# Attention, MoE and a second MoE on one core: w_in with one scale per column half, q and k of the first units as rows of two tokens, two 256-token tiles in a PSUM bank

## The chip, the cores and the metric

The kernel runs on one core of a Trainium2 chip. The metric is the device time of one execution in microseconds; smaller is better. Of several executions the median counts.

## The reference

`reference()` chains three blocks over 3072 tokens. B, H, S, D are 4, 8, 768, 64.

```
for each chunk of 32 queries:                # per batch and head
    k_full = [8 memory keys, k of 16 tokens left, the chunk, 8 tokens right]
    a = softmax(q_c @ k_full.T / sqrt(D));   out_c = a @ v_full
x = out as 3072 x 512
h = x @ w_in                                 # 512 x 2048
g = max(h, 0) + alpha * min(h, 0)
x = g @ w_out                                # 2048 x 512
out = ((x @ w_a) * (x @ w_b)) @ w_out2       # 512 x 1536 twice, 1536 x 512
```

All weights come as 64-bit floating-point numbers in device memory.

## The kernel before, in words

**Weights.** Each weight is loaded as pairs of 32-bit words and rebuilt in f32 on the chip (`chunk`): rebase (L557, L559), shift (L568, L573), magnitude (L579), sign (L587), sizes (L595, L598). Then it is split into a high f16 part (`split_hi`, L370 on POOL or L372 on ACT) and a low f16 part (`split_lo`, L376, always on DVE), both after multiplying by a power of two, the scale. A product of two such pairs takes three f16 matmuls (`gemm3`, L1004 to L1006). w_in comes in 8 chunks of 256 columns, w_out in 8 chunks of 64. All of w_in has one scale, taken from the largest of the 8 chunks' sizes (`scale_w1`, L517); so no chunk of w_in can be split before the last one has its sizes. Each w_out chunk has its own scale. `scale` (L328) turns the sizes with one TensorE transpose (L334) and has four small DVE rows (L339, L343, L347, L350).

**Attention.** 24 units of 128 tokens. For each, SP loads k (L729), q (L777) and v (L791); a row of q or k is one token of one head, 256 bytes. TensorE turns k (L733) and q (L805), four f32 transposes of 128x128 each; ACT and DVE copy the keys to `kT` (L668, L670); the scores are L829, their row maximum on DVE L845 (or L835 and L845), the exponentials on ACT L855, the norm L871, the turn of the probabilities L888, their product with the values L902. In the first 8 units the mask is added by TensorE (L820).

**First MoE.** Tokens go in blocks: two of 256 (two units each), then five of 512. `x_block` (L957) scales x and splits it (`xhl`). `gemm1` (L1008) makes, for each of the 16 row tiles m of h, 12 matmuls into one of four PSUM banks `mm`, then g: `below` on ACT (L1028), `both` on DVE (L1031), the high part on ACT (L1037), the low part on DVE (L1040). `gemm2` (L1057) makes the four column tiles of the output, each in four groups of 12 matmuls, one group per quarter of w_out's rows. The columns of tile 3 are w_out chunks 6 and 7.

**The order.** Nothing runs as written: the class `Schedule` collects every operation with an engine, a cost, a rank and the buffers it reads, writes and holds, and `emit` then writes the program by list scheduling on those costs. Each engine executes its instructions in the order in which they were written. Where `emit` foresees TensorE idle for more than 1.5 us it puts dummy matmuls there (`warm`: L354, L881, L1021). Slots limit how far work runs ahead: 4 banks for `mm`, 2 for `pair` (the turns of k, the scores), 3 `raw` and 2 `w32` slots for weights in preparation, 2 each for q, k and v. Chunks 1 to 3 of w_in wait for their scale in the buffer of g (`ghl`), chunks 4 to 7 in that of w_out (`w_96` in the rows of the order).

**After phase 1** the second MoE follows with a scheme of seven products per 2x2 block of matrices; the change does not touch it.

Of the kernel before, what the change touches and what calls it, by code (L numbers as in the profile page):

```python
# [8 lines left out]
F32 = mybir.dt.float32  # L9
# [10 lines left out]
P = 128  # L20
# [192 lines left out]
def tile_attention_moe_moe2(  # L213
# [81 lines left out]
    s_w1, inv_w1 = col(), col()  # L295
# [204 lines left out]
    in_x, in_g = Buf(raw_slots), Buf(ghl_slots)  # L500

# [13 lines left out]
    am_w1, am1_w1 = col(NC1), col()  # L515

    def scale_w1(rank):  # L517


        def largest():  # L520
            nc.vector.tensor_reduce(out=am1_w1, in_=am_w1, axis=AX.X, op=ALU.max)

        sd.op("DVE", took["largest"], rank, largest, [("amw1", c) for c in range(NC1)], [("amw1", -1)])
        after = [
            lambda: nc.vector.tensor_tensor(out=iy0, in0=als, in1=inv_w1, op=ALU.mult),
            lambda: nc.vector.tensor_scalar(iy0, iy0, 1.0 / E1, None, op0=ALU.mult),
        ]
        scale(lambda: am1_w1, s_w1, inv_w1, [("amw1", -1), ("alpha", 0)], [("s_w1", 0)], after=after)

    def chunk(nm, c, w, kt, cw, rank, load_rank):  # L530
# [32 lines left out]
        def shifted(e):  # L563
# [8 lines left out]
            b = b.rearrange("p (g f) -> p g f", g=2 * kt) if nm == "w1" else b  # L572
# [46 lines left out]
        def scaled():  # L619
            src = [rk, ("s_w1", 0)] if nm == "w1" else [(w32, 0), (key + "s", 0)]  # L620
            if nm in ("w1", "w2"):
                wh, wl = (w1h, w1l) if nm == "w1" else (w2h, w2l)
# [4 lines left out]

                def hi_(e):
                    split_hi(f(), wh[:, :, cols], s, e)

                def lo_():
                    split_lo(f(), wh[:, :, cols], wl[:, :, cols], s)
# [76 lines left out]

    def keys(iu, rank):  # L710
# [3 lines left out]
        kw, pk = Buf(kw_slots), Buf(pair_slots)  # L714
# [31 lines left out]
        sd.op("SP", 1.5, max(iu - 1, 0) * 2.0 + (0.05 if iu else 0.0), load, (), [(kw, 0)])  # L746
        sd.op("PE", 4 * pe(P, 2), rank - 5000, turn, [(kw, 0)], [(pk, 0)])
# [10 lines left out]
    def attention(iu, b, u, x32, part, am, rank):  # L758
# [6 lines left out]
        qt, vw = Buf(qt_slots), Buf(vw_slots)  # L765
# [9 lines left out]
        def load_q():  # L775
            t0 = 2 * u * QB
            nc.sync.dma_start(out=qt.tile, in_=q[b, :, t0 : t0 + P, :].rearrange("h p d -> p h d"))  # L777
# [19 lines left out]
        sd.op("SP", 1.5, lr, load_q, (), [(qt, 0)])  # L797
# [5 lines left out]
        def q_turn():  # L803
            for g in range(HP):
# [113 lines left out]
        sd.op("PE", 4 * pe(P, 2), prank, q_turn, [(qt, 0)], [(pq, 0)], holds=[qT])  # L918
# [38 lines left out]
    def x_block(jb, x32, xhl, c0, rank):  # L957
# [9 lines left out]
        def largest():  # L967
# [15 lines left out]
            [(f"sx{jb}", 0), ("s_w1", 0)], [(f"iy{jb}", 0)],  # L983
# [15 lines left out]
    def gemm3(ps, ops, first=True, last=True):  # L999
# [3 lines left out]
        for i, (lh, ll, rh, rl) in enumerate(ops):  # L1003
            nc.tensor.matmul(out=ps, lhsT=lh, rhs=rh, start=first and i == 0, stop=False)  # L1004
# [139 lines left out]
    for jb, (x32, xhl, ghl, c0, ar, r1, r2) in enumerate(place):  # L1144
# [3 lines left out]
        for m in range(KF1):  # L1148
            gemm1(jb, m, xhl, ghl, c0, n, r1)
# [337 lines left out]
```

## Time and profile before

| | |
|---|---|
| median of 3 runs | 1159.72 us (1158.94 to 1162.37) |
| profiled execution | 1160.92 us, span 1159.1 us, mean granted clock 0.989 |
| TensorE busy | 1124.0 us, 97% of the span, 9253 matmuls |
| DVE busy | 846.7 us, 73% |
| ACT busy | 569.6 us, 49% |
| POOL busy | 279.8 us, 24% |
| DMA | 147.83 MB, 128 GB/s over the span |

The profile is one execution, so its own time is the one to which sums of its rows belong; the span is the part of it that the trace covers. An engine's share of the span is a mean over stages which differ: attention and weight preparation in the first 180 us, matmuls alone later.

### The profile page before, as it was taken

How to read it: one execution, taken by the hardware profiler on the slowest of the kernel's cores; microseconds unless marked ns; L12 is line 12 of the kernel's file. 1: busy time of each engine (PE TensorE's matmuls, PEld its weight loads, DVE VectorE, ACT ScalarE, POOL GpSimd, SP SyncE). 2: the span in 40 equal slices, each digit the busy share in tenths (PEclk: the TensorE clock that was granted, in tenths of full speed). 3: DMA queues.
4: the chain of work that ended last, by engine and by line, in shares of the span. 5: the costliest groups of instructions: out<-in, count | busy, mean ns of one | idle time of the engine just before them, and what ended most of it. 6: DMA issues, size and time to landing. Idle time of an engine off the chain costs nothing.

```text
span 1159.1 us, 22903 instructions
## 1 busy us (share of the span) xinstructions
PE 1124.0 (97%) x9253; PEld 807.8 (70%) x9253; DVE 846.7 (73%) x1472; ACT 569.6 (49%) x1263; POOL 279.8 (24%) x339
## 2 busy tenths in 40 slices
PE   5688999999999999999999999999999999999998
PEld 3477886555555545444444588888888888888887
DVE  5899898877787789654352287976976967958982
ACT  4878767866686676444141122533433433424340
POOL 3432632112112202301200010323332342332610
PEclk9789999999999999999999999999999999999999
DMA  9847655536636543461103162612613504505301
GB/s 269 239 96 172 159 138 151 164 90 184 196 96 170 171 138 99 157 250 46 46 1 136 49 202 68 203 54 101 207 41 115 189 26 146 165 19 177 97 36 38
DMA packets 149874, 147.83 MB, mean 128 GB/s; under 512 B 91385, under 2 KB 127241, under 8 KB 149769
## 3 DMA queue, kind: packets, MB, share of 16 engines
q1 hardware_dynamic: 149768, 146.37, 41.5%
q8 instruction: 73, 1.20, 0.4%
q14 instruction: 33, 0.26, 0.1%
HBM read 117.25 MB, written 29.10 MB: 126 GB/s over the span
## 4 chain that ended last, share of the span: by engine, by line
PE 86%; DVE 9%; ACT 2%; POOL 1%; issue 1%; SPq 1%; DMA 0%; ACTq 0%; DVEq 0%; POOLq 0%
PE mm L1004 27%; PE mm L1006 27%; PE mm L1005 27%; PE mm L902 2%; PE pair L888 2%; DVE w L376 1%; PE pair L829 1%; DVE w L579 1%; DVE w L587 1%; POOL w L370 1%; DVE g L1031 1%; PE mm L805 1%; DVE ghl L1040 1%; PE pair L733 1%; ACT sm L855 1%
## 5 line engine op out<-in xcount | busy, mean ns | idle before, releaser
L1004 PE MATMUL mm<-xhl,w 128*128 128x512 f16 (+1 forms) x448 | 157.6, 352 | 4.3 <-DVE g L1031 3.7
L1005 PE MATMUL mm<-xhl,w 128*128 128x512 f16 (+1 forms) x448 | 157.5, 352 | 1.9 <-DVE xhl L376 1.9
L1006 PE MATMUL mm<-xhl,w 128*128 128x512 f16 (+1 forms) x448 | 157.6, 352 | 0.0
L1004 PE MATMUL mm<-ghl,w 128*128 128x512 f16 (+1 forms) x448 | 156.3, 349 | 0.0
L1006 PE MATMUL mm<-ghl,w 128*128 128x512 f16 (+1 forms) x448 | 156.2, 349 | 0.0
L1005 PE MATMUL mm<-ghl,w 128*128 128x512 f16 (+1 forms) x448 | 156.2, 349 | 0.0
L1004 PE MATMUL mm<-units,w1b 128*128 128x256 f16 x560 | 152.6, 273 | 0.0
L1006 PE MATMUL mm<-units,w1b 128*128 128x256 f16 x560 | 152.6, 273 | 0.0
L1005 PE MATMUL mm<-units,w1b 128*128 128x256 f16 x560 | 152.6, 273 | 0.0
L1006 PEld LDWEIGHTS <-w 128*128 128x128 f16 x896 | 88.1, 98 | 81.1 <-issue 2.1
L1005 PEld LDWEIGHTS <-w 128*128 128x128 f16 x896 | 88.2, 98 | 78.1 <-issue 5.0
L1004 PEld LDWEIGHTS <-w 128*128 128x128 f16 x896 | 88.4, 99 | 75.2
L1005 PE MATMUL mm<-w2b,w1b 128*128 128x256 f16 x504 | 137.4, 273 | 0.0
L1004 PE MATMUL mm<-w2b,w1b 128*128 128x256 f16 x504 | 137.4, 273 | 0.0
L1006 PE MATMUL mm<-w2b,w1b 128*128 128x256 f16 x504 | 137.4, 273 | 0.0
L1004 PEld LDWEIGHTS <-w1b 128*128 128x128 f16 x1064 | 104.1, 98 | 12.1
L1006 PEld LDWEIGHTS <-w1b 128*128 128x128 f16 x1064 | 104.1, 98 | 12.1
L1005 PEld LDWEIGHTS <-w1b 128*128 128x128 f16 x1064 | 104.1, 98 | 12.1
L1031 DVE SCALAR_TENSOR_TENSOR g<-g,columns,mm 128x512 f32<-128x512 f32 (+1 forms) x112 | 73.7, 666 | 26.0 <-ACT g L1028 25.9
L1028 ACT ACTIVATE g<-mm 128x512 f32<-128x512 f32 (+1 forms) x112 | 59.4, 536 | 63.1 <-PE mm L1006 61.7
L1040 DVE SCALAR_TENSOR_TENSOR ghl<-g,ghl 128x512 f16<-128x512 f32 (+1 forms) x112 | 70.2, 637 | 25.3 <-ACT ghl L1037 24.8
L1037 ACT ACTIVATE ghl<-g 128x512 f16<-128x512 f32 (+1 forms) x112 | 62.5, 569 | 30.9 <-DVE g L1031 30.6
(306 smaller groups left out, 2339.0 us busy)
## 6 DMA issues: line engine op xcount, KB each, us to landing
w1b<-wa_d SPq DMA_DIRECT2D x26, 896.0 KB
w1b<-wb_d SPq DMA_DIRECT2D x26, 896.0 KB
raw<-in_moe_w_out_dram SPq DMA_DIRECT2D x8, 1024.0 KB
vw<-in_v_dram SPq DMA_DIRECT2D x40, 176.0 KB
kw<-in_k_dram SPq DMA_DIRECT2D x24, 256.0 KB
qt<-in_q_dram SPq DMA_DIRECT2D x24, 256.0 KB
raw<-in_moe_w_a_dram SPq DMA_DIRECT2D x12, 512.0 KB
raw<-in_moe_w_b_dram SPq DMA_DIRECT2D x12, 512.0 KB
```

Of the source, the lines that this page charges most:

```text
L370: nc.gpsimd.tensor_scalar(hi, src, s, None, op0=ALU.mult)
L376: nc.vector.scalar_tensor_tensor(out=lo, in0=src, scalar=s, in1=hi, op0=ALU.mult, op1=ALU.subtract)
L579: nc.vector.scalar_tensor_tensor(out=f, in0=a, scalar=3 if by["e"] == "ACT" else 29, in1=b, op0=ALU.logical_shift_left if by["e"] == "ACT" ...
L888: nc.tensor.transpose(out=heads(pp, P)[:KW, o, g], in_=sm.tile[:, o, g], identity=ident)
L902: nc.tensor.matmul(out=out[64 * o : 64 * o + 64, g, c], lhsT=vw.tile[:, j, 2 * g + o], rhs=pT.tile[:, o, g, c], start=True, stop=True,)
L1004: nc.tensor.matmul(out=ps, lhsT=lh, rhs=rh, start=first and i == 0, stop=False)
L1005: nc.tensor.matmul(out=ps, lhsT=lh, rhs=rl, start=False, stop=False)
L1006: nc.tensor.matmul(out=ps, lhsT=ll, rhs=rh, start=False, stop=last and i == n - 1)
L1028: nc.scalar.activation(out=g.tile[:, :n], in_=ps.tile[:, :n], func=ACTF.Relu, scale=-1.0)
L1031: nc.vector.scalar_tensor_tensor(out=g.tile[:, :n], in0=g.tile[:, :n], scalar=fal[:, m : m + 1], in1=ps.tile[:, :n], op0=ALU.mult, op1=ALU ...
L1037: nc.scalar.activation(out=ghl.tile[:, 0, m, d], in_=g.tile[:, :n], func=ACTF.Copy, scale=E1)
L1040: nc.vector.scalar_tensor_tensor(out=ghl.tile[:, 1, m, d], in0=g.tile[:, :n], scalar=E1, in1=ghl.tile[:, 0, m, d], op0=ALU.mult, op1=ALU.s ...
```

## The change

Four things, all in the first phase.

(a) w_in gets two scales, one for each half of its columns (4 chunks each). `scale_w1` makes both; four small DVE rows (`ratios`) form r_w1, what each half's scale lacks to the common one. Each w_out chunk multiplies its own scale by r_w1 (one small DVE row, L656 of the new kernel), and its rows are split in two halves, each with its own factor: two high parts and two low parts of 512 per chunk for one each of 1024.

(b) The f16 parts of w_in are stored chunk by chunk (`w1c`) and those of w_out by column tile (`w2m`), so that one chunk's write is contiguous where it was 8 pieces of 128.

(c) q and k of units 0 to 3 are loaded as rows of two tokens, 512 bytes, into 64 partitions of two `raw` slots (`load_wide`), one slot for two units. `turn_wide` turns them with 16 ordinary f32 matmuls with an identity of 64x64 each, where there were four transposes of 128x128; the output goes to every second column of PSUM, even and odd tokens apart.

(d) In the two blocks of 256 tokens two row tiles m share a PSUM bank (`gemm1_pair`): one `below`, one high part on ACT and one low part on DVE for each pair, 512 wide; `both` stays at 256 because its factor differs by m.

The core of the diff:

```diff
-    s_w1, inv_w1 = col(), col()
+    s_w1, inv_w1, r_w1 = col(2), col(2), col(2)
-    w1h, w1l = w1.rearrange("p (x k f) -> x p k f", x=2, k=KD)
+    w1c = w1.rearrange("p (c x k f) -> c x p k f", c=NC1, x=2, k=KD)
-    w2h, w2l = w2.rearrange("p (x k f) -> x p k f", x=2, k=KF1)
+    w2m = w2.rearrange("p (m x k f) -> m x p k f", m=KD, x=2, k=KF1)
...
+        for h in range(2):
+            def largest(h=h):
+                nc.vector.tensor_reduce(
+                    out=am1_w1[:, h : h + 1], in_=am_w1[:, h * NH : (h + 1) * NH], axis=AX.X, op=ALU.max
+                )
...
+            scale(
+                lambda h=h: am1_w1[:, h : h + 1], s_w1[:, h : h + 1], inv_w1[:, h : h + 1],
+                [("amw1", -1 - h)], [("s_w1", h)],
+            )
+        def ratios():
+            nc.vector.tensor_reduce(out=imax, in_=inv_w1, axis=AX.X, op=ALU.max)
+            nc.vector.reciprocal(out=smin, in_=imax)
+            nc.vector.tensor_scalar(r_w1, inv_w1, smin, None, op0=ALU.mult)
+            nc.vector.tensor_scalar(iy0, imax, als, 1.0 / E1, op0=ALU.mult, op1=ALU.mult)
...
+                halves = [(slice(0, kt), s)] if nm == "w1" else [(slice(0, kt // 2), sr[:, :1]), (slice(kt // 2, kt), sr[:, 1:])]
                 def lo_():
-                    split_lo(f(), wh[:, :, cols], wl[:, :, cols], s)
+                    for ks, x in halves:
+                        split_lo(f()[:, ks], wh[:, ks], wl[:, ks], x)
+                        lambda: nc.vector.tensor_scalar(sr, r_w1, s, None, op0=ALU.mult),
...
+    def load_wide(i, src, iu):
+        (t, r), (b, u) = wide(iu, i), units[iu]
+        nc.sync.dma_start(
+            out=t[r].rearrange("p h e d -> p h (e d)"),
+            in_=src[b, :, u * P : (u + 1) * P, :].rearrange("h (p e) d -> p h (e d)", e=2),
+        )
+    def turn_wide(i, out, iu):
+        t, r = wide(iu, i)
+        out = out.rearrange("p (g t e) -> p g t e", g=HP, e=2)
+        for g in range(HP):
+            for e in range(2):
+                for o in range(2):
+                    nc.tensor.matmul(
+                        out=out[64 * o : 64 * o + 64, g, :, e], lhsT=t[r, 2 * g + o, e], rhs=ident[r, r],
+                        start=True, stop=True,
+                    )
...
-        sd.op("SP", 1.5, lr, load_q, (), [(qt, 0)])
+        sd.op("SP", 0.8 if iu < 4 else 1.5, lr, load_q, (), [qkey])
...
+    def gemm1_pair(jb, m, xhl, ghl, c0, rank):
+        for x in range(2):
+            def product(x=x, c=c, wh=wh, wl=wl):
+                xh, xl = xhl.tile[:, 0, :, d], xhl.tile[:, 1, :, d]
+                gemm3(
+                    halves(ps.tile)[:, x], [(wh[:, i, c], wl[:, i, c], xh[:, i, :], xl[:, i, :]) for i in range(KD)],
+                    first=x == 0, more=True,
+                )
+        sd.op("ACT", act(TB), er, below, [(ps, 0)], [(g, 0), (g, 1)])
+        for x in range(2):
+            sd.op("DVE", dve(HT, pointers=1), er, lambda x=x: both(x), [(ps, 0), ("alpha", 0)], [(g, x)])
+        sd.op("ACT", act(TB), er, hi_, [(g, 0), (g, 1)], [(ghl, ("h", m, c0))])
+        sd.op("DVE", dve(TB), er, lo_, [(g, 0), (g, 1), (ghl, ("h", m, c0))], [(ghl, (m + x, c0)) for x in range(2)], port=True)
```

Since `emit` sets the order from costs and slots, the whole order of the first phase shifts. Three places of it follow; the rows are instructions of one engine in program order, with the line, the operation, the tiles and the shape, and x16 for sixteen of them in a row.

TensorE, from the turn of unit 0's probabilities (L888, now L947) to unit 1's scores (L829, now L888); before:

```order
L888 MATMUL pair<-ident,sm 96x128 x8
L902 MATMUL mm<-pT,vw 64x64 x16
L805 MATMUL mm<-ident,qt 128x128 x4
L733 MATMUL pair<-ident,kw 128x128 x4
L820 LDWEIGHTS ident_92
L820 MATMUL pair<-mask_90,ident_92 128x384
L820 LDWEIGHTS ident_92
L820 MATMUL pair<-mask_90,ident_92 128x384
L829 MATMUL pair<-kT,qT 64x96 x16
```

and in the changed kernel:

```order
L947 MATMUL pair<-ident,sm 96x128 x8
L754 MATMUL mm<-ident,raw 64x64 x16
L961 MATMUL mm<-pT,vw 64x64 x16
L754 MATMUL pair<-ident,raw 64x64 x16
L879 LDWEIGHTS ident_92
L879 MATMUL pair<-mask_90,ident_92 128x384
L879 LDWEIGHTS ident_92
L879 MATMUL pair<-mask_90,ident_92 128x384
L888 MATMUL pair<-kT,qT 64x96 x16
```

The turn of q for unit 1 stood behind the product with the values and stands ahead of it now; the turn of k for unit 2 stays ahead of unit 1's scores. Four transposes have become sixteen matmuls in both.

DVE, around the row maximum of unit 1 (`nm`); before:

```order
L911 TENSOR_REDUCE columns<-x_302 128x1
L587 SCALAR_TENSOR_TENSOR ghl<-ghl,w_95 128x1024
L668 COPY kT<-pair 128x4x80
L587 SCALAR_TENSOR_TENSOR ghl<-ghl,w_95 128x1024
L845 TENSOR_REDUCE nm<-pair 128x8
L568 TENSOR_SCALAR w_95<-w_95 128x8x128
L579 SCALAR_TENSOR_TENSOR w_95<-w_96,w_95 128x8x128
```

and in the changed kernel, up to the first rows of the next chunk:

```order
L970 TENSOR_REDUCE columns<-x_353 128x1
L695 COPY kT<-pair 128x4x16
L695 COPY kT<-pair 128x4x8
L602 SCALAR_TENSOR_TENSOR ghl<-ghl,w_95 128x1024 x2
L904 TENSOR_REDUCE nm<-pair 128x8
L526 TENSOR_REDUCE columns<-columns 128x1
L340 TENSOR_REDUCE m<-mm 128x1
L344 TENSOR_SCALAR m<-m 128x1
L348 TENSOR_SCALAR columns<-m 128x1
L351 RECIPROCAL columns<-columns 128x1
L584 TENSOR_SCALAR w_95<-w_95 128x1024
L594 SCALAR_TENSOR_TENSOR w_95<-w_96,w_95 128x1024
```

The two signs of w_in chunks (L587, now L602) stand next to each other ahead of the maximum, behind the copies of the keys. Behind the maximum come the largest size of w_in's first half (L526) and the rows of its scale (L340 to L351); before, the one scale of w_in stands behind the first xhl.

DVE, the end of w_out: the last chunks' low parts (`w_96` is the buffer of w_out, with numbered tiles as sources); before:

```order
L350 RECIPROCAL columns<-columns 128x1
L668 COPY kT<-pair 128x4x72
L602 COPY columns<-columns 64x1
L668 COPY kT<-pair 128x4x8
L1076 TENSOR_TENSOR columns<-columns 128x1 x2
L376 SCALAR_TENSOR_TENSOR w_96<-w_1801,columns,w_96 128x16x64
L376 SCALAR_TENSOR_TENSOR w_96<-w_1854,columns,w_96 128x16x64
```

and in the changed kernel:

```order
L351 RECIPROCAL columns<-columns 128x1
L617 COPY columns<-columns 64x1
L1192 TENSOR_TENSOR columns<-columns 128x1 x2
L656 TENSOR_SCALAR columns<-columns 128x2
L584 TENSOR_SCALAR w_2092<-w_2092 128x1024
L594 SCALAR_TENSOR_TENSOR w_2092<-raw,w_2092 128x1024
L970 TENSOR_REDUCE columns<-x_1365 128x1
L377 SCALAR_TENSOR_TENSOR w_96<-w_1938,columns,w_96 128x8x64 x2
```

The low parts of the last two chunks stood next to each other, 1024 each (16x64). Now the last chunk stands alone, in two halves of 512 (8x64), with a shift and a magnitude (L584, L594) of the next weight and a row of sizes (L970) between its factor (L656) and its low part. On POOL the order has 14 of the long operations on weights (L370, L557) up to there where it had 18.

## Rows read from the trace of the kernel before

**Rows 1.** Page, busy tenths in 40 slices; then windows: busy us and instructions per engine.

```profile
PE   5688999999999999999999999999999999999998
...
59.00:180.00 121.00, 112.00 (x1263) 94.83 (x1263) 112.04 (x236) 93.36 (x268) 49.70 (x28) 0.97 0.56 137
180.00:240.00 60.00, 60.00 (x520) 35.36 (x517) 49.12 (x86) 45.35 (x120) 6.95 (x11) 1.00 0.56 156
```

**Rows 2.** Waits, TensorE 59 to 180 us, DVE 33 to 160 us: total, times, longest.

```profile
PE mm L1004 <- DVE g L1031: 3.7, 2, 2.8
PE mm L1005 <- DVE xhl L376: 1.9, 1, 1.9
...
DVE w L376 <- POOL w L370: 2.2, 3, 1.0
...
DVE w L376 <- ACT w L372: 0.8, 1, 0.8
```

**Rows 3.** Chain that ended last, pieces in order: start us, us, what.

```profile
8.80 3.98 DMA kw<-in_k_dram
...
154.21 2.85 POOL w L370
157.09 2.48 DVE w L376 x2
```

**Rows 4.** Timeline of TensorE at 160.7 us: start us, us, instruction.

```profile
160.72 0.27 PE L1004 MATMUL mm<-ghl,w 128*128 128x256 f16 x1
```

**Rows 5.** DMA traffic from 0 to 20 us in slices of half a microsecond.

```profile
GB/s 0 0 0 14 88 156 217 340 397 381 375 299 276 267 209 184 184 190 115 75 203 264 195 186 271 336 397 373 389 385 397 401 401 393 385 389 393 389 385 382
```

**Rows 6.** Timeline of TensorE, 12 to 45 us; in brackets the idle time before.

```profile
12.83 1.12 PE L733 MATMUL pair<-ident,kw 128*128 128x128 f32 x4 [2.10 <-DMA kw<-in_k_dram]
...
15.43 1.54 PE L829 MATMUL pair<-kT,qT 64*64 64x96 f32 x28 [0.33 <-DVE kT L668]
...
25.80 2.57 PE L902 MATMUL mm<-pT,vw 96*64 96x64 f32 x32 [0.78 <-DVE pT L668]
...
43.11 1.98 PE L902 MATMUL mm<-pT,vw 96*64 96x64 f32 x32 [1.39 <-ACT pT L670]
```

**Rows 7.** Timeline of DVE, row maxima of units 0 and 1, one scale.

```profile
17.03 0.96 DVE L845 TENSOR_REDUCE nm<-pair 128x8 f32<-128x768 f32 x1 [1.65 <-PE pair L829]
...
33.05 0.96 DVE L845 TENSOR_REDUCE nm<-pair 128x8 f32<-128x768 f32 x1 [0.23 <-PE pair L829]
...
53.87 0.29 DVE L339 TENSOR_REDUCE m<-mm 128x1 f32<-128x128 f32 x1 [0.42 <-PE mm L334]
```

**Rows 8.** DVE timeline; then groups by form, busy us, mean ns; DVE, then ACT.

```profile
10.97 1.21 DVE L587 SCALAR_TENSOR_TENSOR raw<-raw,w 128x1024 int32<-128x1024 int32 x1
...
19.88 2.01 DVE L587 SCALAR_TENSOR_TENSOR ghl<-ghl,w 128x1024 int32<-128x1024 int32 x1
...
82.24 0.75 DVE L1040 SCALAR_TENSOR_TENSOR ghl<-g,ghl 128x256 f16<-128x256 f32 x2
...
L1040 DVE SCALAR_TENSOR_TENSOR ghl<-g,ghl 128x512 f16<-128x512 f32 x80 | 56.3, 711 | 24.9 <-ACT ghl L1037 24.4
...
L376 DVE SCALAR_TENSOR_TENSOR xhl<-x,columns,xhl 128x512 f16<-128x512 f32 x24 | 17.4, 766 | 0.0
...
L376 DVE SCALAR_TENSOR_TENSOR w<-w,columns,w 128x1024 f16<-128x1024 f32 x12 | 16.3, 1376 | 2.2 <-POOL w L370 1.5 <-ACT w L372 0.8
...
L1040 DVE SCALAR_TENSOR_TENSOR ghl<-g,ghl 128x256 f16<-128x256 f32 x32 | 13.9, 451 | 0.4 <-ACT ghl L1037 0.4
...
L568 DVE TENSOR_SCALAR w<-w 128x1024 int32<-128x1024 int32 x14 | 10.0, 714 | 1.1 <-ACT w L559 1.1
...
L343 DVE TENSOR_SCALAR m<-m 128x1 int32<-128x1 int32 x47 | 7.1, 151 | 1.1
...
L372 ACT ACTIVATE w<-w,columns 128x1024 f16<-128x1024 f32 x5 | 6.0, 1217 | 0.7 <-DVE columns L350 0.7
```

**Rows 9.** Group of TensorE by form: busy us, mean ns of one.

```profile
L829 PE MATMUL pair<-kT,qT 64*64 64x96 f32 x768 | 24.5, 260 | 1.4 <-ACT kT L670 0.9 <-DVE kT L668 0.3
```

More of the change, by code (lines that the diff above doesn't have):

```diff
@@ L500, in tile_attention_moe_moe2 @@
     in_x, in_g = Buf(raw_slots), Buf(ghl_slots)
+    wide_qk = [Buf(raw_slots) for _ in range(2)]
     def raw_key(c):
@@ L513, in raw_tile @@
         return t[:, c * n : (c + 1) * n].bitcast(I32).rearrange("p (f t) -> p f t", t=2)
-    am_w1, am1_w1 = col(NC1), col()
+    am_w1, am1_w1 = col(NC1), col(2)
+    NH = NC1 // 2
     def scale_w1(rank):
[L520 to L528, printed above, removed]
+        for h in range(2):
[3 more added lines that the diff above has]
+                )
+            sd.op(
+                "DVE", took["largest"], rank, largest, [("amw1", c) for c in range(h * NH, (h + 1) * NH)],
+                [("amw1", -1 - h)],
+            )
[8 more added lines that the diff above has]
+            nc.vector.tensor_scalar(iy0, imax, als, 1.0 / E1, op0=ALU.mult, op1=ALU.mult)
+        sd.op("DVE", 4 * took["tiny"], rank, ratios, [("s_w1", 0), ("s_w1", 1), ("alpha", 0)], [("r_w1", 0)])
     def chunk(nm, c, w, kt, cw, rank, load_rank):
@@ L997, in x_block, with gemm3 @@
         return iy
[L999 removed]
+    def gemm3(ps, ops, first=True, last=True, more=False):
         n = len(ops)
         for i, (lh, ll, rh, rl) in enumerate(ops):
[L1004 to L1006 removed]
+            nc.tensor.matmul(out=ps, lhsT=lh, rhs=rh, start=first and i == 0, stop=False, skip_group_check=more)
+            nc.tensor.matmul(out=ps, lhsT=lh, rhs=rl, start=False, stop=False, skip_group_check=more)
+            nc.tensor.matmul(out=ps, lhsT=ll, rhs=rh, start=False, stop=last and i == n - 1, skip_group_check=more)
     def gemm1(jb, m, xhl, ghl, c0, n, rank):
         ps, g = Buf(mm_slots), Buf(g_slots)
[L1010 removed]
+        c = slice(m % GR * P, (m % GR + 1) * P)
+        wh, wl = w1c[m // GR, 0], w1c[m // GR, 1]
         d = slice(c0, c0 + n)
@@ L1016, in product @@
                 ps.tile[:, :n],
-                [(w1h[:, i, c], w1l[:, i, c], xh[:, i, :], xl[:, i, :]) for i in range(KD)],
+                [(wh[:, i, c], wl[:, i, c], xh[:, i, :], xl[:, i, :]) for i in range(KD)],
             )
@@ L1147, in tile_attention_moe_moe2 @@
         iy = x_block(jb, x32, xhl, c0, ar)
-        for m in range(KF1):
-            gemm1(jb, m, xhl, ghl, c0, n, r1)
+        for m in range(0, KF1, 2 if n == HT else 1):
+            if n == HT:
+                gemm1_pair(jb, m, xhl, ghl, c0, r1)
+            else:
+                gemm1(jb, m, xhl, ghl, c0, n, r1)
         for m in range(KD):
```

86 lines of the change are left out of this document (68 added, 18 removed).

## The prediction

> **What bounds the kernel now.** I read the stretches of the span first, since the share of busy time hides the stages [rows 1]. From 180 us on TensorE hardly pauses: 60.00 us busy of 60, and nine tenths or more in every later slice of the span but the last. So whatever the change does, it must do by bringing TensorE's work before 180 us to an earlier or later end. Between 59 and 180 us TensorE is busy 112.00 of 121 us, so 9.0 us of idle time is all that can be won there; DVE is busy 112.04 us in the same stretch, so it is as full as TensorE.
>
> The waits and the chain name the links. From 59 to 180 us the products of the first GEMM wait 3.7 us for g and 1.9 us for xhl, both written by DVE. DVE in turn waits, from 33 to 160 us, 2.2 us for POOL's and 0.8 us for ACT's rounding of weights [rows 2]. The chain that ended last runs at its front through the load of k (8.80 to 12.83 us), and before GEMM2's last column block through POOL's rounding of a w_out chunk (2.85 us) and DVE's two low parts behind it, which end at 157.09 + 2.48 = 159.57 us [rows 3]. The first product that needs them, by the order the 577th of the two GEMMs, starts at 160.72 us [rows 4]. So only 1.1 us lies between the end of the weights' preparation and their use: TensorE's stream and DVE's w_out chain are both critical, and a gain on one is worth little more than 1 us without the other. That decides the forecast.
>
> I split the change at two marks: N, the row maximum of unit 1 on DVE (33.05 us in the rows), and M, the first product with the last two w_out chunks (160.72 us).
>
> **Part 1: loads and turns of q and k, up to N.** The wide loads move the same 256 KB each. While the narrow ones run, the DMA moves 184 to 209 GB/s, and with w_in alone 373 to 401 [rows 5]: 256 KB are 1.40 us at 187 and 0.68 us at 385, so each gains 0.7 us. By the order three of them (k0, q0, k1) lie ahead of unit 0's scores, 2.1 us together. The turns for k1 started 2.10 us late for that load, but the maximum of unit 0 had DVE idle only 1.65 us [rows 6, 7], and DVE had other work for the rest: I take 1.65 us as the gain. The trace shows no 512-byte row into 64 partitions; if such rows ran no faster than the narrow ones, the gain would be nothing, and that is the upper bound below.
>
> Against that, a turn was 4 transposes, 1.12 us at this stage; it is now 16 ordinary f32 products that write every second column. The nearest rows are 16 f32 products of the attention, which the trace records as 32: 1.54 us for 28 records of the scores (1.76 for 32), and 1.98 and 2.57 us for the values [rows 6]. So a turn costs 0.3 us more (half of the early 0.64) to 1.45 us more; I take +0.9, the 1.98 of the values less 1.12. Exposed are three: k1, and q1 and k2, which the new order puts ahead of unit 1's scores as the old one did; the others lie in gaps that dummy products fill in the order of today. N: 3 x 0.9 - 1.65 = **+1.05 us** (bounds: 3 x 0.3 - 1.65 = -0.75; with no gain from the loads 3 x 1.45 = +4.35). On SP the loads keep their places, so nothing is overtaken there.
>
> **Part 2: DVE from N to the last w_out low part.** Counted from the order up to that low part, priced by [rows 7, 8]:
> - a second scale for w_in, one maximum over 128 values and four tiny rows: 0.29 + 4 x 0.15 = +0.9; the ratios, 4 tiny rows in place of 2: +0.3; one tiny row for each of the 8 w_out chunks: +1.2.
> - w_out's low parts in halves: 16 x 0.766 (the 512-wide xhl row) for 8 x 1.376: +1.25.
> - three shifts that go from ACT to DVE: 3 x 0.714 = +2.1.
> - g's low parts in pairs: 16 x 0.711 for 32 x 0.451, -3.05; back to back two of 256 took 0.75 us, which would make it -0.6. I take the middle, -1.8. `both` stays at 32 of 256.
> - four long POOL operations fewer (18 to 14 of about 2.9 us, as the one in the chain). DVE's `signed` (L587) took 2.01 us beside one, 1.21 us without: -3.2; at worst 0.
>
> Sum **+0.75 us** (bounds -0.5 and +5.2). The order also moves bit operations of the last w_out chunk and sends fewer splits to POOL, so that waits for the rounding (3.0 us in all) should shrink: I take -2.2, POOL's part (bounds -3.0 and 0).
>
> **Part 3: M itself.** M's first products run over the first half of w_out's rows. The new low part is in two halves, so they wait for the first only: the second low half (0.77) and the second half of the rounding (about half of ACT's 1.2) fall away, **-1.4 us** (bounds -1.4 and 0). The one wait that comes in is on r_w1: chunks of w_out cannot be rounded before both halves of w_in have their scales. That they could not before either: the store of w_out's parts holds chunks 4 to 7 of w_in until these are split. So I price it at nothing; were it exposed, it would cost one wait like that for the transpose of the sizes (0.42) [rows 7].
>
> **At nothing:** the chunk-wise storage of w_in and w_out (the same 1024 elements per row of DVE); ACT's below and hi in pairs (ACT is busy 93 of 121 us, behind TensorE and DVE); the scale per half, which lets four w_in chunks be split earlier but leaves the first GEMM behind all eight wide turns and behind xhl, as the order shows; and the shared PSUM bank: 12 products more before a bank is evacuated, 8 banks fewer to claim, covered by the w_out chain.
>
> **Sum:** 1.05 + 0.75 - 2.2 - 1.4 = -1.8 us. The rows are of one execution, 1160.92 us with a span of 1159.1; the median of the runs is 1159.72, 1.2 us below it. So 1159.1 against the profiled run, **1158.0** against the median. A measurement of this kernel can tell about 0.3% (3.5 us) from no change; this is inside it.
>
> **The rivals.**
> *Faster: TensorE's stream leads, not w_out.* Then the pairs count: a product group has one evacuation where it had two, and the waits for g and xhl (5.6 us) vanish, while DVE fills its own idle time to keep the low parts of w_out in front. Price: +1.05 - 5.6 = -4.55, that is 1155.2; with all 9.0 us of idle time gone, 1151.8. For it: DVE has 9.0 us idle from 59 to 180 us, all in small waits. Against it: each of them has a cause, and a DVE that is busy 112 of 121 us must lose nearly all. Chance 0.38.
>
> *Slower: the wide turns are long.* The 16 products of a turn write PSUM with a gap of one element, which no product of the kernel before does. One record of the scores lasts 0.26 us by the mean of its group [rows 9]; if 16 products do not overlap at all, a turn takes 4.2 us in place of 1.12, N comes 3 x 3.1 - 1.65 = +7.6 us late, and the sum is 7.6 + 0.75 - 2.2 - 1.4 = +4.8: 1164.5. It decides from 3.8 us per turn. For it: nothing hides k1, q1 and k2. Against it: the values, 64 rows by 64 columns too, take 1.98 to 2.57. The Trainium skill, page "PSUM — Partial Sum Buffer", section "Specifications (TRN2)", says that any non-contiguous access slows products significantly; no run here shows such an access yet, so the chance stands on the rows alone, and by the rule the time would be this rival's. Chance 0.13.
>
> *Slower: the w_out chain ends late.* If POOL's rest gives DVE nothing and no wait goes, part 2 is +5.2 and the sum 1.05 + 5.2 - 1.4 = +4.85: 1164.6. It decides from M more than 3.5 us later. Chance 0.09.
>
> *It doesn't do what it says.* The half scale is meant to let the split of w_in begin early; where the first GEMM still waits for xhl, that is worth nothing. This is already inside the forecast.
>
> **How the numbers follow.** The forecast has 0.40, and its own range is within 3.5 us of the median. The faster rival has 0.38, the two slower ones 0.22. The range goes from 1150 (below the 1151.8 of all idle time) to 1166 (above 1164.6); what it leaves out is turns longer than 4.2 us both slower rivals at once, and unforeseen gains.
>
> **What would show it.** Right: the wide loads at 0.7 us less each; a wide turn at 1.5 to 2.6 us early; N at 33 to 35 us; the second scale behind N; the pairs' low part at 0.71 us; M at 157 to 162 us, with the last low half less than 1.5 us ahead of it; TensorE without pause from there. Wrong: M earlier than 156 us with TensorE waiting for neither g nor xhl (first rival), or a wide turn of 3.8 us and more (second), or TensorE idle in front of M behind a w_out low part (third).

## The result, and the profile after

The changed kernel takes 1167.45 us (median of 5 runs, 1165.34 to 1170.9), the kernel before 1160.27 in the same comparison. The ratio is 1.0065, with a 95% interval of 1.0051 to 1.0079: slower by 7 us, beyond the 0.3% that counts as no change, and above the forecast's range. The profiled execution took 1168.8 us with a span of 1167.0; the rows below belong to it, 7.9 us against the 1160.92 and 1159.1 before.

First the page's slices and the windows of the changed kernel; columns as in [rows 1].

```profile
PE   5789999999999999999999999999999999999998
...
59.00:180.00 121.00, 109.70 (x1199) 91.12 (x1198) 114.15 (x251) 94.15 (x250) 33.13 (x22) 0.97 0.60 147
180.00:240.00 60.00, 59.72 (x533) 37.06 (x533) 46.92 (x82) 46.17 (x123) 11.76 (x17) 1.00 0.53 152
36.20:168.30 132.10, 115.59 (x1278) 93.19 (x1278) 120.97 (x251) 101.73 (x264) 40.98 (x25) 0.91 0.67 162
```

From 180 us on TensorE has no pause, as before; the 7.9 us are lost ahead of that. N, the row maximum of unit 1, and M, the 577th product, are the marks of the prediction. N came at 36.22 us for 33.05, M at 168.58 for 160.72: +3.2 and, behind N, another +4.7. From N to the end of the last low part of w_out DVE was busy 120.97 of 132.10 us. The same stretch before:

```profile
33.00:159.60 126.60, 109.44 (x1183) 88.39 (x1182) 115.55 (x232) 101.34 (x296) 51.31 (x24) 0.93 0.65 160
```

DVE works 5.4 us more, and its idle time is 11.1 us in both. So the forecast's part 2 was too small, and DVE's idle time, of which it took 2.2 us away, stayed as long.

The DMA traffic of the first 20 us in slices of half a microsecond, as in [rows 5]:

```profile
GB/s 0 0 0 17 61 156 205 369 406 401 402 310 191 119 124 185 169 183 135 127 107 170 129 176 271 207 176 155 159 205 348 393 389 389 381 385 393 385 410 360
```

Where the wide q and k of the first units run (6 to 9 us) it moves 119 to 191 GB/s, 162 in the mean; the same stretch before, with the narrow ones, has 184 to 276, 218 in the mean [rows 5]. The chain that ended last, at its front (start, us, what):

```profile
8.64 1.76 SPq L743
...
22.48 8.04 DMA raw<-in_k_dram
...
33.11 3.20 DVE ghl L602 x2
```

The issue of k1 alone keeps SP 1.76 us (0.49 us for the narrow load), and k2, in unit 1's way, is 8.04 us from its issue to its landing. Then TensorE, in three places, with the idle time before a row in brackets:

```profile
9.46 1.97 PE L754 MATMUL pair<-ident,raw 64*64 64x64 f32 x32 [0.17 <-DMA raw<-in_k_dram]
...
15.52 1.98 PE L754 MATMUL pair<-ident,raw 64*64 64x64 f32 x32 [2.38 <-DMA raw<-in_k_dram]
...
27.10 1.15 PE L754 MATMUL mm<-ident,raw 64*64 64x64 f32 x32
28.18 1.52 PE L961 MATMUL mm<-pT,vw 96*64 96x64 f32 x32
30.66 1.33 PE L754 MATMUL pair<-ident,raw 64*64 64x64 f32 x32 [0.96 <-DMA raw<-in_k_dram]
...
48.30 1.97 PE L754 MATMUL mm<-ident,raw 64*64 64x64 f32 x32
50.21 1.97 PE L961 MATMUL mm<-pT,vw 96*64 96x64 f32 x32
```

The turn for k1 starts at 15.52 us for 12.83 [rows 6]; k2's waits 0.96 us more. A wide turn takes 1.97 us at the early pace and 1.15 later. The pace goes with the granted clock: at 27.10 us it is 1.00 (2.4 GHz), behind dummy matmuls, and the turn takes 1.15 us; at 48.30 it is 0.50 (1.2 GHz) and the turn takes 1.97, as does the product with the values (L961) at 50.21. The maxima of units 0 and 1 on DVE, and the two signs between:

```profile
20.58 0.96 DVE L904 TENSOR_REDUCE nm<-pair 128x8 f32<-128x768 f32 x1 [1.65 <-PE pair L888]
...
33.02 3.27 DVE L602 SCALAR_TENSOR_TENSOR ghl<-ghl,w 128x1024 int32<-128x1024 int32 x2
36.22 0.94 DVE L904 TENSOR_REDUCE nm<-pair 128x8 f32<-128x768 f32 x1
```

The two signs took 3.27 us where two cost 2.4 alone (2 x 1.21 [rows 8]). At M:

```profile
166.89 1.40 DVE L377 SCALAR_TENSOR_TENSOR w<-w,columns,w 128x512 f16<-128x512 f32 x2
...
168.42 0.32 PE L335 MATMUL mm<-ident,columns 128*128 128x128 f32 x1 [0.46 <-DVE columns L1027]
168.58 0.27 PE L1063 MATMUL mm<-ghl,w 128*128 128x256 f16 x1
```

The last low half ends at 166.89 + 1.40 = 168.29 us, 0.3 us ahead of the product. TensorE is idle for 0.46 us just before, until a small row of DVE (L1027) that stands behind the low halves. As before, the w_out chain and TensorE arrive together, both late. TensorE's waits from 59 to 185 us and DVE's from 36 to 168 us (total, times, longest):

```profile
PE mm L335 <- ACT raw L613: 3.9, 5, 1.3
PE mm L1127 <- ACT qT L871: 2.6, 1, 2.6
PE mm L1064 <- DVE xhl L377: 1.9, 1, 1.9
...
PE mm L1063 <- DVE g L1153: 0.3, 1, 0.3
...
DVE m L340 <- PE mm L335: 1.6, 2, 1.1
DVE kT L695 <- PE pair L787: 1.5, 2, 1.1
...
DVE w L377 <- POOL w L371: 0.7, 2, 0.4
```

The wait for g shrank from 3.7 to 0.3 us [rows 2], and that for POOL from 2.2 to 0.7, so parts of the change did what they say. Others came in their place. TensorE waits 3.9 us for ACT's sizes of weights (L613) and 2.6 us for ACT's copy of qT, where it waited 1.3 and 0.6 us before; DVE waits 5.6 us for TensorE in all, where it waited 1.4. DVE's groups between N and the last low part, by form (busy, mean ns, idle before); the last row is one of the kernel before, from 33.0 to 159.6 us:

```profile
L377 DVE SCALAR_TENSOR_TENSOR w<-w,columns,w 128x512 f16<-128x512 f32 x16 | 13.0, 850 | 0.7 <-POOL w L371 0.7
...
L1162 DVE SCALAR_TENSOR_TENSOR ghl<-g,ghl 128x512 f16<-128x512 f32 x16 | 11.1, 701 | 0.6 <-ACT ghl L1159 0.4
...
L602 DVE SCALAR_TENSOR_TENSOR w<-raw,w 128x1024 int32<-128x1024 int32 x8 | 10.2, 1282 | 0.0
...
L594 DVE SCALAR_TENSOR_TENSOR w<-w,w 128x1024 int32<-128x1024 int32 x4 | 6.6, 1662 | 0.5 <-ACT w L588 0.5
...
L602 DVE SCALAR_TENSOR_TENSOR w<-w,w 128x1024 int32<-128x1024 int32 x4 | 5.7, 1418 | 0.0
...
L584 DVE TENSOR_SCALAR w<-w 128x1024 int32<-128x1024 int32 x6 | 5.0, 828 | 0.3 <-ACT w L575 0.2
...
L656 DVE TENSOR_SCALAR columns<-columns 128x2 f32<-128x2 f32 x8 | 1.8, 240 | 0.0
...
L579 DVE SCALAR_TENSOR_TENSOR w<-w,w 128x1024 int32<-128x1024 int32 x4 | 4.9, 1222 | 1.1 <-ACT w L573 1.0
```

### The profile page after: what moved, and what is told of

Read it like the earlier page. It is cut to its first block, busy times and chain, and to the rows that moved or that the text cites. A ratio compares the mean times of both kernels' runs of the same rounds, so it can differ in the third digit from the quotient of the medians.

```text
span 1167.0 us, 23342 instructions
## 1 busy us (share of the span) xinstructions
PE 1130.8 (97%) x9482; PEld 814.4 (70%) x9482; DVE 847.6 (73%) x1484; ACT 569.9 (49%) x1237; POOL 265.5 (23%) x339
## 3 DMA queue, kind: packets, MB, share of 16 engines
q8 instruction: 74, 1.21, 0.4%
## 4 chain that ended last, share of the span: by engine, by line
PE 86%; DVE 7%; ACT 2%; DMA 2%; SPq 1%; issue 1%; POOL 0%; ACTq 0%; POOLq 0%
PE mm L1063 26%; PE mm L1064 26%; PE mm L1065 26%; PE mm L961 2%; PE pair L947 1%; PE pair L888 1%; DVE w L594 1%; DVE w L602 1%; DVE w L377 1%; DVE g L1153 1%; DMA wb_d<-sp 1%; SPq L846 1%; DMA raw<-in_k_dram 1%; DVE ghl L1162 1%; PE mm L864 1%
## 5 line engine op out<-in xcount | busy, mean ns | idle before, releaser
L1091 DVE SCALAR_TENSOR_TENSOR g<-g,columns,mm 128x512 f32<-128x512 f32 x80 | 59.2, 743 | 25.4 <-ACT g L1088 25.2
L1088 ACT ACTIVATE g<-mm 128x512 f32<-128x512 f32 x80 | 47.4, 593 | 61.4 <-PE mm L1065 61.3
L1063 PE MATMUL mm<-units,ghl 128*128 128x256 f16 x280 | 76.3, 273 | 0.0
L1065 PE MATMUL mm<-units,ghl 128*128 128x256 f16 x280 | 76.3, 273 | 0.0
```

The source lines that it names most:

```text
L1065: nc.tensor.matmul(out=ps, lhsT=ll, rhs=rh, start=False, stop=last and i == n - 1, skip_group_check=more)
L1088: nc.scalar.activation(out=g.tile[:, :n], in_=ps.tile[:, :n], func=ACTF.Relu, scale=-1.0)
L1091: nc.vector.scalar_tensor_tensor(out=g.tile[:, :n], in0=g.tile[:, :n], scalar=fal[:, m : m + 1], in1=ps.tile[:, :n], op0=ALU.mult, op1=ALU ...
```

## The experiments

Three theories. **A**: the wide q and k are the loss. **B**: the halves (two scales of w_in, w_out's parts in two) are. **C**: the pairs, the storage or the new order as such. Times are medians; each ratio is to runs of the kernel before made beside it, whose medians were 1160.2 to 1160.8 us.

**e1: everything but the wide q and k.**

```diff
-    wide_qk = [Buf(raw_slots) for _ in range(2)]
+    wide_qk = []
...
-            if iu < 4:
+            if iu < 0:
...
```

> The change with the narrow loads and the transposes of q and k put back; scale halves, chunk-wise storage and pairs stay. Theory A (the wide q and k are the loss: they land late and their turns take about 2.0 us at the half clock): unit 1's row maximum returns from 36.2 to about 33 us and the time falls by 5 to 7 us to 1160-1162. Theory B (the halves of w_in and w_out are the loss, by DVE work between that maximum and the last low part of w_out, 132.1 us in place of 126.5): the maximum returns to 33 us, but the 132 us stay, and the time falls by 3 us at most, to 1164-1167.

Measured 1164.79 us, ratio 1.0037 (1.0024 to 1.0051). N returned to 32.80 us, but the time fell by only 2.7 us. B is right for this part: without the wide loads 4 us of loss remain.

**e2: nothing but the wide q and k**, put into the kernel before (`load_wide`, `turn_wide` and what calls them).

> The kernel before with nothing but the wide loads and turns of units 0 to 3. Theory A: 1164 to 1167, 4 to 7 us over the kernel before, row maximum of unit 1 at 36 us. Theory B: at most 3 us over, 1160 to 1163.

1166.14 us, ratio 1.0047 (1.0030 to 1.0063), N at 36.27 us. A holds as well. Both losses are real.

**e3: one scale, w_out's parts in one piece; the rest of the change stays.**

```diff
-    NH = NC1 // 2
+    NH = NC1
...
-        for h in range(2):
+        for h in range(1):
...
-                halves = [(slice(0, kt), s)] if nm == "w1" else [(slice(0, kt // 2), sr[:, :1]), (slice(kt // 2, kt), sr[:, 1:])]
+                halves = [(slice(0, kt), s)]
...
```

> The change with one scale for w_in and w_out's parts in one piece of 1024; wide q and k, chunk-wise storage and pairs stay. Theory A: 1165 to 1168, as the change; from the maximum of unit 1 to the last low part of w_out about 132 us again. Theory B: 1161 to 1164; that stretch falls back to 126 to 128 us.

1165.85 us, ratio 1.0043 (1.0027 to 1.0058): the wide q and k alone again, with pairs and storage. The time is as theory A has it, the stretch is not: from N to the last low part of w_out it is 120.8 us where A had 132 and B 126 to 128. The last low part, and M:

```profile
156.11 1.28 DVE L377 SCALAR_TENSOR_TENSOR w<-w,columns,w 128x1024 f16<-128x1024 f32 x1
...
165.63 0.27 PE L1053 MATMUL mm<-ghl,w 128*128 128x256 f16 x1
```

The w_out chain is through at 157.4 us, 8.2 us ahead of the product that needs it, and the loss is there all the same. In e3 it is not the end of w_out that makes TensorE late.

**e5, e6, e7: the other parts on narrow q and k.** e5 is e3's edit upon e1; e7 also drops the pairs; e6 is e1 without the pairs:

```diff
-        for m in range(0, KF1, 2 if n == HT else 1):
-            if n == HT:
+        for m in range(0, KF1, 1):
+            if False:
```

> Only the pairs and the chunk-wise storage: narrow q and k, one scale of w_in, w_out's parts in pieces of 1024. Theory B (the halves make the 4 us that remained without the wide loads): within 1.5 us of the kernel before, 1159 to 1162, and from the row maximum of unit 1 to the last low part of w_out 126 to 128 us. Theory C (the pairs or the new order, not the halves): 1163 to 1166.

> Only the halves (two scales of w_in, w_out's parts in two pieces) and the chunk-wise storage: narrow q and k, no pairs. Theory B: 1164 to 1167, the stretch from the maximum of unit 1 to the last low part of w_out 131 us or more (the low parts of g in 32 pieces again cost DVE 3 us more than in the kernel without the wide loads). Theory C: 1160 to 1162.

> Only the chunk-wise storage. Both theories: within 1.5 us of the kernel before, 1159 to 1162; DVE's rows on weights keep 1.2 to 1.3 us for 1024. If it is slower by 3 us or more, the order that the planner makes of small differences is itself the cause.

e5 gave 1160.31 us, ratio 0.9996 (0.9986 to 1.0005); e6 1164.26, 1.0035 (1.0024 to 1.0046); e7 1159.66, 0.9995 (0.9986 to 1.0005). Storage and pairs change nothing and C falls. The stretch from N to the last low part of w_out is 131.3 us in e1, 128.2 in e6 (131 or more was expected) and 120.0 in e5 (126 to 128 was expected). With e3 it shows that this stretch does not go with the time. The losses add up almost, 0.0080 for 0.0065:

| | one scale | halves |
|---|---|---|
| narrow q and k | 0.9996 (e5) | 1.0037 (e1) |
| wide q and k | 1.0043 (e3) | 1.0065 (the change) |

The intervals of e3 and of the change overlap (1.0027 to 1.0058 and 1.0051 to 1.0079): what the halves add on top of the wide loads is less sure than what they cost alone.

### Why the wide loads are slow

**e4: the same rows of 512 bytes, but two units per load into all 128 partitions.**

```diff
-            out=t[r].rearrange("p h e d -> p h (e d)"),
-            in_=src[b, :, u * P : (u + 1) * P, :].rearrange("h (p e) d -> p h (e d)", e=2),
+            out=t.rearrange("p h e d -> p h (e d)"),
+            in_=src[b, :, u * P : (u + 2) * P, :].rearrange("h (p e) d -> p h (e d)", e=2),
...
```

> The change with one load of 512 KB into all 128 partitions for two units at a time (same rows of 512 bytes, same layout in the chip, same turns). If writing 64 partitions only is what holds the wide loads at 110 to 190 GB/s, these four loads move at 300 GB/s and more, the turn of k for unit 1 starts by 12.5 us where it started at 15.5, and the time falls by 2 to 4 us. If rows of 512 bytes are no better than 256 here, or the loads are held by their place behind w_in, the turn stays at 15 us and the time within 1 us of the change.

1163.34 us, ratio 1.0028 (1.0010 to 1.0046). The median hides two groups: five executions of 1160.3 to 1161.8 us, with a mean granted clock of 0.995 to 0.997, and five of 1164.9 to 1167.0 us, at 0.988 to 0.993. The trace is of the first group (1161.76 us). There the loads run at 261 to 311 GB/s and N is back at 32.60 us. It still has the halves. What makes the two groups is open.

**e9, e12 and e17: e4's loads without the halves**; in e12 and e17 each load in two by heads, so that a load has 256 KB as in the change.

```diff
+        for h in (slice(0, HP), slice(HP, H)):
+            nc.sync.dma_start(
+                out=t[:, h].rearrange("p h e d -> p h (e d)"),
+                in_=src[b, h, u * P : (u + 2) * P, :].rearrange("h (p e) d -> p h (e d)", e=2),
+            )
...
```

> The version that the runs point to: loads of q and k into all 128 partitions for two units at a time with the wide turns, pairs and chunk-wise storage, but one scale of w_in and w_out's parts in one piece. If the slow loads and the halves are all of the loss, it is at least as fast as the kernel before: 1156 to 1160. If the wide turns themselves cost time, 1162 or more.

> As e9, each load in two of 256 KB, by heads, still into 128 partitions. If the partitions set the rate, q and k move at 260 GB/s and more as in e4, with the same size of 256 KB as in the change; if it was the size of a load, they fall to 130 to 180. Time within 2 us of e9.

> e12 timed: wide q and k by loads of 256 KB into 128 partitions, pairs, chunk-wise storage, no halves. If the faster loads win what they save (0.5 to 0.7 us each, three ahead of unit 0's scores) net of the longer turns: 1158 to 1160, at most 2 us below the kernel before. If the turns eat it: the same as the kernel before within 1 us.

e9: 1160.35 us, ratio 0.9994 (0.9985 to 1.0002). e12: one execution, 1159.02 us. e17, the same kernel timed: 1160.26 us, ratio 1.0002 (0.9993 to 1.0010). The DMA traffic of e12 from 0 to 20 us:

```profile
GB/s 0 0 0 17 78 135 205 373 393 393 379 300 303 333 308 293 280 299 275 173 156 172 172 189 232 324 381 385 385 393 406 365 377 393 389 397 385 393 389 381
```

Rows of 512 bytes in loads of 256 KB move at 275 to 333 GB/s (5.5 to 9.5 us; 225 to 326 in e17) when they go to 128 partitions, and at 119 to 191 (6 to 9 us) when they go to 64. From 6 to 9 us the means are 303 and 276 GB/s in e12 and e17 for 162 in the change. So it is the number of partitions, neither the row nor the size of a load. The Trainium skill, page "SBUF — State Buffer", section "Door 1: The DMA port swizzle (why `[64,N]` ≈ `[32,N]`)", says that a transfer's rate depends on how many of 16 ports its partitions reach, and that partition numbers which differ by 64 are on different ports; 64 in a row reach half of them, and the trace agrees, with about half the rate. e9 keeps all the wide turns and costs nothing against e5: the turns are not the loss, the slow loads are. Nor do the faster loads win anything: e17 is within 1 us of the kernel before, the second branch of its expectation. Its scores of unit 1 end at 30.2 us for 33.0 before, but N comes at 33.02 us for 33.05, because DVE is busy without a pause from 21.0 us up to it, mostly with rows of w_in.

**e8: the wide turns without the gap in PSUM.** The tokens of units 0 to 3 then stand in another order, so their results are others.

```diff
-        out = out.rearrange("p (g t e) -> p g t e", g=HP, e=2)
+        out = out.rearrange("p (g e t) -> p g t e", g=HP, e=2)
```

> The change with the wide turns writing even and odd tokens of a unit into two contiguous halves of PSUM instead of every second column (the tokens of units 0 to 3 then stand in another order, which changes what is computed for them). If the gap costs, a turn takes clearly less than the 1.97 us early and 1.15 us later that it has now; if the price is that of 16 f32 products, as the product with the values has it, the same 1.97 and 1.15, and the time within 2 us of the change.

One execution, 1168.54 us. Two of its turns:

```profile
9.97 1.97 PE L754 MATMUL pair<-ident,raw 64*64 64x64 f32 x32
...
27.28 1.15 PE L754 MATMUL mm<-ident,raw 64*64 64x64 f32 x32
```

1.97 and 1.15 us, to the hundredth what they take with the gap. The Trainium skill, page "PSUM — Partial Sum Buffer", section "Specifications (TRN2)", has any non-contiguous access slow products down significantly; for f32 products that write 64 columns with a gap of one element the measurement says otherwise, and it decides.

**e14: the change planned with the truth.** The planner took 0.8 us for a wide load; here it takes 2.0.

```diff
-        sd.op("SP", 0.8 if iu < 4 else 1.5, lr, load_q, (), [qkey])
+        sd.op("SP", 2.0 if iu < 4 else 1.5, lr, load_q, (), [qkey])
...
```

> The change with the planner's cost of a wide load raised from 0.8 to 2.0 us; the instructions are the same, their order is planned anew. If the loss comes from a plan on a load time that is not kept: 3 us or more faster than the change, 1164 or less. If the slow loads lose by themselves: within 2 us of the change, 1165.5 to 1169.

1168.83 us, ratio 1.0059 (1.0044 to 1.0074), the same as the change: an order planned on the longer loads does not save them.

### Why the halves lose

**e10 and e11: one kind of halves at a time**, with e5's other parts. In e10 w_out keeps one piece and its own scale, and the factor of the halves is left out; in e11 w_in has one scale and both factors are one.

> Of the halves only the two scales of w_in, with pairs, chunk-wise storage, narrow q and k; w_out's parts in one piece with their own scale and without the factor of the halves (left out). If the early split of w_in's first half is what hurts (four low parts ahead of xhl): 1163 to 1166. If it is DVE's added work on w_out: 1159 to 1161.

> Of the halves only w_out's parts in two pieces with a factor for each (here one, as w_in has one scale), with pairs, chunk-wise storage, narrow q and k. If DVE's added work on w_out hurts (8 factors, 16 low parts of 512 for 8 of 1024: some 4 us): 1162 to 1165. If it is the early split of w_in: 1159 to 1161.

e10: 1163.02 us, ratio 1.0020 (1.0009 to 1.0032). e11: 1161.16 us, ratio 1.0007 (0.9997 to 1.0018), not told apart from no change. The two scales of w_in alone cost 2.3 us by their ratio; e11 lies between its two expectations. The intervals of e10 and e11 overlap, so that the scales make the larger part of e1's 1.0037 is likely, not shown.

What the halves do with narrow loads can be read in e1 against e5. Products of the first GEMM and of GEMM2 begun by a time:

| us | 80 | 90 | 100 | 110 |
|---|---|---|---|---|
| e5 (one scale) | 120 | 167 | 204 | 275 |
| e1 (halves) | 150 | 192 | 204 | 239 |

With the halves TensorE is 25 products ahead at 90 us, has lost that at 100 and is 36 behind at 110. Its timeline in e1, and the row on DVE that ends the stop:

```profile
91.59 0.29 PE L335 MATMUL mm<-ident,columns 128*128 128x128 f32 x1 [2.50 <-DVE columns L1027]
96.50 0.40 PE L1063 MATMUL mm<-ghl,w 128*128 128x256 f16 x1 [4.62 <-POOL w L371]
...
98.41 0.42 PE L1065 MATMUL mm<-ghl,w 128*128 128x256 f16 x1
...
101.08 0.37 PE L1064 MATMUL mm<-xhl,w 128*128 128x256 f16 x1 [0.54 <-DVE xhl L377]
...
98.78 2.24 DVE L377 SCALAR_TENSOR_TENSOR xhl<-x,columns,xhl 128x512 f16<-128x512 f32 x2
```

Block 0's 192 products of the first GEMM are through (the last starts at 85.79 us), and nothing else is ready: a chunk of w_out is not rounded yet (4.62 us of waiting for POOL, which starts on it at 93.88), and xhl of block 1 is complete only at 98.78 + 2.24 = 101.0 us. The products behind the stop take 0.42 us each, at the lower clock (the granted clock is 0.50 of full from 92.3 to 102.6 us). In e5, where the 192nd product starts at 92.71 us, xhl of block 1 is complete at 96.4 us:

```profile
95.63 0.74 DVE L377 SCALAR_TENSOR_TENSOR xhl<-x,columns,xhl 128x512 f16<-128x512 f32 x1
```

The windows of e1, then of e5 (columns as in [rows 1]):

```profile
33.00:90.00 57.00, 46.80 (x469) 35.38 (x469) 54.40 (x102) 47.38 (x120) 28.80 (x14) 0.91 0.75 181
90.00:120.00 30.00, 22.07 (x237) 17.79 (x238) 27.52 (x67) 22.91 (x66) 9.62 (x6) 0.83 0.61 143
120.00:180.00 60.00, 57.36 (x626) 49.42 (x623) 54.90 (x117) 46.54 (x122) 18.64 (x16) 1.00 0.57 157
```

```profile
33.00:90.00 57.00, 45.97 (x467) 33.84 (x460) 51.54 (x85) 47.12 (x131) 23.38 (x10) 0.89 0.74 174
90.00:120.00 30.00, 26.41 (x302) 21.36 (x303) 28.93 (x63) 25.38 (x68) 16.23 (x6) 1.00 0.59 147
120.00:180.00 60.00, 58.23 (x681) 51.03 (x670) 53.77 (x114) 44.35 (x117) 16.29 (x15) 1.00 0.57 146
```

DVE is all but full up to 90 us in e1: 54.40 of 57 us, 2.9 us more than in e5. It splits w_in early, ahead of xhl, and so, as I read it, brings forward the work for block 0's products; unit 3's row maximum is at 69.31 us for 66.92, and block 1 follows. From 90 to 120 us TensorE is busy 22.07 us (clock 0.83) for 26.41 (clock 1.00), 4.3 us less, and from 120 to 180 us it does not make it good (57.36 for 58.23). The two profiled spans are 3.8 us apart. By the 288th product e1 is 4.3 us behind (115.67 for 111.41), at the 289th only 0.7, since e5 waits longer for that one, and at the 577th 3.7: the number of a product is a rough mark, since the two orders place the attention between the products differently. e10 has the same stop: its 192nd product starts at 87.01 us and its 193rd at 95.98.

Two things limit this account. In the changed kernel itself there is no such stop and no lead: its 192nd product starts at 102.70 us, for 94.47 before, and the 193rd at 102.81. How the halves add to the late loads there is not shown. And e4 has the halves, a lead, and no loss in its profiled execution. Its 192nd product starts at 88.62 us, for 96.25 in e9, which has the same loads without the halves; its xhl of block 1 is complete at 92.27 + 1.41 = 93.68 us, and the next product starts with it:

```profile
92.27 1.41 DVE L377 SCALAR_TENSOR_TENSOR xhl<-x,columns,xhl 128x512 f16<-128x512 f32 x2
...
93.68 0.27 PE L1068 MATMUL mm<-xhl,w 128*128 128x256 f16 x1
```

From the 192nd product to the next it takes 5.1 us where e1 takes 10.7, and M comes at 160.56 us. So the halves need not lose. That the place of block 1's xhl decides is a reading of these traces, not shown; the five longer executions of e4 have no trace.

**e13: no stop for the clock.** 14 dummy products ahead of GEMM2's first.

```diff
+            if jb == 0 and m == 0 and i == 0:
+                for _ in range(14):
+                    nc.tensor.matmul(
+                        out=ps.tile.rearrange("p (g t) -> p g t", g=HP), lhsT=ident16,
+                        rhs=ident16[:, None, :].to_broadcast([P, HP, P]), start=True, stop=True,
+                    )
```

> e1 (halves, pairs, storage, narrow q and k) with 14 dummy products on TensorE ahead of GEMM2's first product, where it waits 4.6 us. If the lower clock behind that wait is part of the loss, the 20 products that took 0.42 us each take 0.27 and the time falls by 2 us against e1, to 1162.5 or less. If the end of w_out's chain sets the time, it stays within 1 us of e1.

1164.69 us, ratio 1.0032 (1.0019 to 1.0044): as e1. The clock did what was asked, and the time did not:

```profile
92.15 4.87 PE L1183 MATMUL mm<-ident 128*128 128x512 bf16 x14
96.94 0.28 PE L1063 MATMUL mm<-ghl,w 128*128 128x256 f16 x1
...
101.49 0.27 PE L1064 MATMUL mm<-xhl,w 128*128 128x256 f16 x1 [1.78 <-DVE xhl L377]
```

The products take 0.27 us again, and then TensorE waits 1.8 us for the same xhl. At this stop the lower clock is a companion, not the price.

**e15, e16, e18: the second MoE's weights held back** until w_out is done, in e1, e5 and e17.

```diff
-        sd.op("SP", dma(n * 8 * P), load_rank, load, (), [rk])
+        sd.op("SP", dma(n * 8 * P), load_rank, load, [(f"w2{NR - 1}", 0)] if pair else (), [rk])
```

> e1 with the loads of the second MoE's weights held back until the last low part of w_out is planned, so that DVE does none of that work before it. If that work ahead of w_out costs: the last low part of w_out ends at 160 us or before (164.1 in e1) and the time falls by 3 us or more, to 1162 or less. If not: within 1.5 us of e1.

> e5 (pairs and storage alone) with the same hold. There the last low part of w_out ended at 153.8 us, 7 us ahead of the product that needs it, so nothing should be won: 1159 to 1162.

> The same with the second MoE's weights held back as in e16: within 1 us of e17.

e15: 1165.13 us, ratio 1.0035 (1.0023 to 1.0047). The last low part of w_out ends at 161.1 us for 164.1, and the time stays: TensorE reaches M at 165.54 us, 4.4 us behind it, for 164.41 in e1. e16: 1159.53 us, ratio 0.9989 (0.9980 to 0.9999). e18: 1158.96 us, ratio 0.9990 (0.9981 to 0.9999), 1.3 us below e17 where at most 1 was expected. Among these runs the two have the lowest ratios, by 0.1%: pairs and chunk-wise storage with the hold, with either kind of q and k, but one scale. That is inside what I called no change.

## Why the prediction was wrong

- **Part 1, the loads.** This is the first step that failed. "Each gains 0.7 us" took the rate of w_in's loads, which go to 128 partitions, as the price of a wide row, and "no faster than the narrow ones" as the worst. They were slower: k1's turn began 2.7 us later instead of 1.65 us earlier. I had written that the trace shows no 512-byte row into 64 partitions, and still allowed no loss. N came +3.2 us for the +1.05 of the sum; within its bounds (-0.75 to +4.35), but by another cause. The turns were priced right: 1.97 us where 1.98 was taken, and e8 says that the gap costs nothing.
- **"At nothing: the scale per half".** The second step that failed. I judged the early split by the first GEMM's start, which it does not bring forward much, and by DVE's sum of rows, which it does not change. With narrow loads the halves cost 4 us (e1, e6). There the order within a full DVE counted: TensorE had its first 192 products 7 us earlier than in e5 and then stood still (e1, e10). Storage and pairs were rightly at nothing (e5, e7).
- **The path: DVE's w_out chain to M.** The sum runs from N over DVE's rows to M. In e3, e5 and e9 the last low part ends at 157.4, 153.8 and 148.6 us, 8.2, 7.0 and 14.2 us ahead of M, and nothing is won by it: one loses, two are as the kernel before. So TensorE's own stream set the time in them, and the sum over DVE's rows does not give it; in the change the two still met within 0.3 us. M itself is a rough mark: in e9 it comes at 162.84 us, 2.1 later than before, and the time is that of the kernel before.
- **Part 2, the ledger of DVE.** Sum +0.75 us, bounds -0.5 to +5.2; DVE's busy time grew by 5.4 us. The pairs' low parts gained 13.9 - 11.1 = 2.8 us (taken: 1.8). The term that failed most is "four long POOL operations fewer, -3.2": the integer rows on weights (magnitude and sign) did not get shorter. They took 1.37 us in the mean, for 1.24 before; the four of L594 from w to w took 1.66, the four of L602 1.42, for 1.22 in both before. The low parts out of ghl alone moved the other way, 1.27 us for 1.88. Low parts of 512 took 0.85 us, not 0.766, the factors 0.24 each, not 0.15, and six shifts stand there for three, as counted.
- **Waits, -2.2 us.** The wait for POOL fell by 1.5 us, but DVE's idle time stayed at 11.1 us: waits for TensorE took its place (5.6 us for 1.4).
- **Part 3, -1.4 us** can't be read from the run: M came 0.3 us behind the last low half, so it is not seen whether the first half alone would have released it. The sum of the parts, against the median, is 1157.9; the 1158.0 is a slip of rounding.
- **The rivals.** The faster one fails by its own test: M came at 168.58 us, not before 156, and TensorE still waited 1.9 us for xhl. The one on long turns is refuted by the turn's 1.97 us and by e8. The third, with w_out's chain late at 1164.6 us, comes nearest in its number, and part 2 did go beyond its +5.2; but TensorE was idle for only 0.46 us in front of M, and e3 loses with that chain 8.2 us ahead. What the range left out, two slower causes at once, is what happened, though neither was one of the two slower rivals.

That a plan on too short a load is to blame is refuted (e14); the lower clock is refuted for e1's stop alone (e13). From 33 to 60 us the granted clock is 0.63 in the change for 0.78 before, and no run separates that from the late loads. What also stays open: why N 3.2 to 3.5 us late becomes 5 us and more at the end (e2, e3), why DVE's rows on weights grew longer in the changed order, and what puts e4 into one or the other of its two groups.

## What to carry to other kernels

Price a load by a row with the same number of partitions, not by the same row length: half the partitions cost about half the rate here, and the doubled row was no compensation. Where one engine is full, doing a part of its work earlier need not be a gain for the engine that waits for it: look at what moves behind, one block further, and at where the lead is spent. And where two steps may fail in the same direction, the range has to hold both at once.

## What the runs showed that was not expected

- From 6 to 9 us, 512-byte rows into 64 partitions: 119 to 191 GB/s; into 128: 225 to 333 (e4, e9, e12, e17); 256-byte rows into 128: 184 to 276 [rows 5].
- f32 products that write every second column of PSUM take as long as those that write side by side: 1.97 us for 16 at the early pace, 1.15 later, in both.
- A kernel whose TensorE runs dummy products through a stop of 4.6 us, so that the products behind take 0.27 us for 0.42, ends no earlier (1164.69 for 1164.79 us).
- The same kernel, e4, ran in two groups 5 us apart, each with its own mean granted clock (0.995 to 0.997, and 0.988 to 0.993).
